# Loading the first two heads of k through SyncE, with a new order of the steps

## The chip, the core and the metric

The kernel runs on one core of one Trainium2 chip. A core has a matrix engine (TensorE, PE in the profile; its weight loads are listed apart as PEld), a vector engine (VectorE, DVE), a scalar engine (ScalarE, ACT), GpSimd (POOL) and SyncE (SP), which only issues transfers here. Each engine works through its own list of instructions in order; semaphores tie the lists together. Transfers are issued by GpSimd or by SyncE and carried by 16 DMA engines. In this kernel the transfers that GpSimd issues also change float32 into bfloat16 on the way.

The metric is the device time of one execution in microseconds (us), lower is better. Times are medians over several runs; the profile is of one execution.

## What is computed

Attention over a window and over block summaries, for 4 batches of 8 heads, 768 positions and 64 numbers a head, and behind it a feed-forward layer on the 3072 resulting rows of 512:

```python
def _attn_ref(q, k, v):
    block, window = (32, 16)
    k_sum = k.reshape(B, H, nb, block, D).max(axis=3)
    v_sum = v.reshape(B, H, nb, block, D).mean(axis=3)
    scores_l = scale * np.matmul(q, k.transpose(0, 1, 3, 2))
    mask_l = np.abs(pos[:, None] - pos[None, :]) < window
    scores_s = scale * np.einsum('bhsd,bhnd->bhsn', q, k_sum) + np.log(block)
    scores_all = np.concatenate([np.where(mask_l, scores_l, -1e9), scores_s], axis=-1)
    a = softmax(scores_all)
    return np.matmul(a, np.concatenate([v, v_sum], axis=2))

def _moe_ref(x, w_in, w_out):
    h = x @ w_in                                   # 512 -> 2048
    return (h * np.clip(h + 3.0, 0.0, 6.0) / 6.0) @ w_out
```

All inputs and the output are float32; the kernel computes in bfloat16 with float32 sums.

## The kernel before, in words

**Work.** The queries of a head are cut into 12 blocks of 64; a block sees a window of 96 keys and 24 block summaries, 120 keys in all. Heads are taken in pairs p = 0 to 3. The feed-forward part works on eight tiles of 384 rows (two halves of each batch): the F groups (line 666) multiply a tile by one of 16 column blocks of `w_in`, four matmuls of 384 columns each; ScalarE and VectorE make the gate from the result (lines 670 and 671); the G groups (line 683) multiply by `w_out`; a copy and a store by SyncE end them (lines 694 and 695).

**An order written out.** The functions only declare steps to a planner, `Plan`, with what each reads and writes. The string `ORDER` then lists every step once, by its key: the tag of the group and a number within it. A suffix `:A` or `:D` puts a step on ScalarE or VectorE. Since each engine's list is in order, this string fixes what stands behind what on every engine. `Plan.issue` walks it, gives each step its buffers (the free one that was released longest ago) and emits the instructions. Tokens that begin with `_`, `-`, `~` or `=` are filler for TensorE, emitted by `keep` (line 771): matmuls on the constant tile `idle` whose result nobody reads. `_40` is 40 matmuls of 64 columns, `-15` is 15 of 128, `~12` is 12 of 512, `=3` is one of 3 x 64 columns.

**The opening of batch 0.** These are the groups that the change and the prediction speak of:

- `c.n`: constants. c.0 is `idle`, c.1 the identity and c.2 the band (both on GpSimd), c.3 the bias for masking (`negative`), c.4 the mask, c.5 the indicator for block sums, c.6 and c.7 edges of `vaug`, c.8 to c.15 zeroed parts of `vaug`, c.16 and c.17 to c.20 edges of the sums and of `kaug`. All but c.1, c.2 and those of c.8 to c.15 that carry `:A` are VectorE's.
- `K00`, `K01`, `K02`: k of head pair 0, of pair 1 and of pairs 2 and 3, loaded by GpSimd into `knat`, a view of the tile `first` (`load_k`, line 303). `Q00`, `Q01`: half of q of pairs 0 and 1, and of 2 and 3 (line 309). `V00` to `V03`: v of one pair each (line 339). `Q0w0` to `Q0w2`: the other half of q, into `qwide` (line 316). `I0`, `I2`, `I4`, `I8`, `I12`: column blocks of `w_in`. `O0` to `O3`: `w_out`.
- `kp.0`: TensorE turns k of pair p by 16 transposes (line 391); `kp.1` takes the block maxima (line 402) and `kp.4` spreads them (line 407), both on VectorE; `kp.2` and `kp.3` copy the turned keys into `kaug`. `q0` and `q1` do the same for q (line 420), `q2` and `q3` for the half in `qwide` (line 441).
- `s0p0.0`: a matmul with the bias that opens the masked scores of pair p, first half of the queries (line 481, "cover"); `s0p0.1` the scores (line 489), `s0p0.2` the exponential. `s0p1` are the scores of the other half, which need `q2` and `q3`.
- `u0`, `u1`: block sums of v for two pairs each (line 535). `h000` and so on (batch, pair, half) are copies of v between blocks. `v0p`: values of pair p (line 581), their division by the sums, transposes (line 589) and the copy into the input tile of the first F groups.

The later batches (1 to 3) are loaded by GpSimd while the feed-forward groups of earlier tiles run. The loads of batch 2 reuse the tile `first`, so `load_raw` makes them wait for the readers of `knat` and `qnat` (`free`, line 337).

`ot` is a pool of four float32 buffers of 128 x 512, from which the output is stored.

Of the kernel before, what the change touches and what calls it, by code (L numbers as in the profile page):

```python
# [15 lines left out]
D = 64  # L16
# [7 lines left out]
RUN = 8  # L24
RP = 96
# [4 lines left out]
c.0 K00.0 c.7 c.17 c.6 c.8:A K01.0 c.10:D c.5 c.1 _40 -15 k0.0 k0.2:A c.18 ~1 =2 k1.0 K02.0 ~12 =3 k2.0 k3.0 c.15:D c.2 c.3  # L30
s000.0 k0.3:A c.13:D c.4 c.11:A k1.1 Q00.0 q0.0 k1.4 k0.1 c.20 k1.2:A Q01.0 ~2 =5 q1.0 k0.4 k1.3:D c.9:A c.14:A c.19 k2.3:A
q0.1:A s000.1 q0.2:A =1 s010.0 s010.1 k2.2:A k3.2:D k3.3:D k3.1 V00.0 h000.0:D h001.0:D k2.1 k2.4 s000.2 ~2 =5 v00.0 V01.0 u0.0
h010.0:D s020.0 c.16 s010.2 q1.2:A u0.3:D u0.1:D u0.4:D v01.0 v01.1 v01.2 v00.1 q1.1:A V02.0 h020.0:A h021.0:A h011.0:A v00.2
s020.1 v01.3 v00.3 V03.0 u1.0 u1.3:A h030.0:D s030.0 k3.4 ~2 s030.1 u1.4:D v01.4 h031.0:D Q0w0.0 Q0w1.0 v01.5:D Q0w2.0 =1 q3.0
q3.1:D q2.0 u1.1:A u1.2:D s020.2 v02.0 v02.1 v02.2 s021.0 v02.3 s030.2 v03.0 v03.1 q2.1:A v03.2 s011.0 v03.3 v00.4 v00.5:D v02.4
s021.1 s011.1 s021.2 v03.4 v03.5:D s011.2 v02.5:A s031.0 s031.1 s001.0 s031.2 I2.0 F0x3.0 F0x3.1 F0x3.2 F0x3.3 F0x3.4 F0x3.5
I4.0 F0x6.0 F0x6.1 F0x6.2 F0x4.0 F0x4.1 F0x4.2 F0x4.3 v411.0 v411.1 F0x5.0 F0x4.4 F0x4.5 v411.2 s001.1 I8.0 u0.2:A s001.2 F0x8.0
F0x8.1 F0x8.2 F0x5.1 I0.0 F0x5.2 F0x11.0 F0x1.0 F0x11.1 F0x11.2 F0x1.1 F0x1.2 F0x1.3 F0x1.4 F0x1.5 v410.0 v410.1 F0x7.0 F0x7.1
F0x7.2 v410.2 F0x10.0 F0x10.1 I12.0 F0x13.0 F0x13.1 F0x15.0 F0x15.1 F0x13.2 F0x10.2 v411.3 v411.4:D v410.3 v410.4:A F0x15.2
F0x14.0 F0x14.1 F0x14.2 F0x9.0 F0x9.1 F0x9.2 F0x0.0 F0x0.1 F0x2.0 F0x2.1 K13.0 K10.0 c.12:A F0x0.2 K12.0 K11.0 w10.0 Q1w1.0  # L40
F1x14.0 F1x14.1 F1x14.2 F1x4.0 F1x4.1 F1x4.2 F1x2.0 F1x2.1 F1x2.2 w10.1:D F0x2.2 F0x2.3 F0x2.4 F0x12.0 F0x12.1 F0x12.2 F1x8.0
F1x8.1 F1x8.2 F1x1.0 F1x1.1 F1x1.2 F0x0.3 F0x0.4 F0x0.5 F0x2.5 F1x9.0 F1x9.1 F1x9.2 F1x5.0 F1x5.1 F1x5.2 F1x15.0 F1x15.1 w11.0
w11.2 F1x15.2 w11.3:D Q1w4.0 Q1w2.0 Q1w0.0 w10.2 w10.3:D q6.0 q6.1:A q7.0 q7.1:A F1x7.0 F1x7.1 w11.1:A F1x7.2 F1x12.0 F1x12.1
F1x12.2 O0.0 G02x0.0 Q1w5.0 Q1w3.0 q4.0 q4.1:A q5.0 q5.1:A F1x6.0 F1x6.1 F1x6.2 O1.0 G02x0.1 s100.0 s100.1 s100.3 F1x3.0 w12.0
F1x11.0 F1x11.1 w13.0 w13.2 F1x3.1 F1x11.2 w12.2 w12.1:D O2.0 G02x0.2 s101.0 s101.1 O3.0 F1x10.0 G02x0.3 G02x0.4:A w13.3:D
w13.1:A s101.3 F1x0.0 G00x0.0 G00x0.1 w12.3:D s100.2 s101.2 s100.4 V10.0 h100.0:D F1x10.1 h110.0:A F1x10.2 F1x3.2 s110.0 s110.1
s110.2 s101.4 s110.3 G00x0.2 G00x0.3 G00x0.4:A V12.0 u4.0 h130.0:D h120.0:A F1x0.1 u4.1:D u4.2:A u4.4:D u4.3:D u4.5:D G02x0.5
G01x0.0 G01x0.1 G01x0.2 s110.4 F1x0.2 h111.0:A v100.0 v100.1 v100.2 h121.0:A v101.0 v101.1 v101.2 G01x0.3 G01x0.4:A K20.0 K21.0
K22.0 K30.0 K23.0 w21.0 F1x13.0 F1x13.1 F1x13.2 v100.3 v100.4:A w20.0 w21.3 G12x0.0 w21.2:A v101.3 v101.4:A V22.0 H2.0 h101.0:A
w20.3 G12x0.1 G12x0.2 F2x2.0 F2x2.1 F2x11.0 F2x2.2 F2x11.1 F2x11.2 s111.0 w23.0 s111.3 F2x1.0 F2x1.1 F2x1.2 F2x3.0 F2x3.1 F2x3.2  # L50
F2x15.0 F2x15.1 F2x15.2 Q22.0 w23.3 G12x0.3 s111.1 G12x0.4:A F2x5.0 F2x5.1 h131.0:A F2x5.2 F2x6.0 G10x0.0 s111.2 w22.0 w22.3
s111.4 w23.4:A V20.0 H2.1:A K33.0 F2x13.0 F2x13.1 F2x13.2 G10x0.1 F2x6.1 F2x0.0 F2x0.1 F2x0.2 u5.0 u5.1:A u5.5:A F2x6.2 v110.0
v111.0 v111.1 v111.2 Q30.0 F2x4.0 F2x4.1 F2x4.2 Q21.0 Q23.0 Q20.0 w22.4:A F2x10.0 F2x10.1 F2x10.2 F2x12.0 F2x12.1 w20.1 F2x12.2
w22.2:A v110.1 w21.4:A Q33.0 Q32.0 G10x0.2 G01x0.5 G10x0.3 G10x0.4:A v110.2 F2x8.0 F2x8.1 w21.1 w20.2:A F2x9.0 w20.4:A F2x9.1
F2x9.2 u5.2:D F2x14.0 u5.4:D w23.2:A F2x8.2 v111.3 F2x14.1 v111.4:A G11x0.0 G11x0.1 u5.3:D w22.1 v110.3 v110.4:A F2x7.0 F2x7.1
G11x0.2 F3x14.0 F3x14.1 F2x14.2 F2x7.2 F3x14.2 s200.0 s200.1 w23.1 w21.5:A s200.3 G11x0.3 F3x9.0 F3x9.1 F3x9.2 F3x8.0 F3x8.1
F3x8.2 F3x13.0 Q31.0 K31.0 s200.4 s200.2 G11x0.4:A G11x0.5 G12x0.5 s210.0 s210.3 s210.4 s210.1 s210.2 F3x4.0 F3x12.0 G22x0.0
F3x13.1 F3x13.2 H3.0 v201.0 K32.0 V32.0 w20.5:D F3x4.1 F3x4.2 V30.0 G00x0.5 F3x12.1 v200.0 v200.1 F3x2.0 v201.1 v201.2 v201.3
G22x0.1 F3x0.0 F3x0.1 G22x0.2 G22x0.3 w23.5:A G22x0.4:A F3x12.2 v200.2 v200.3 v201.5 F3x1.0 F3x1.1 F3x1.2 s201.0 w31.0 G20x0.0
v201.4 F3x0.2 F3x2.1 s201.3 F3x2.2 F3x11.0 s201.1 G20x0.1 F3x5.0 F3x11.1 F3x3.0 F3x5.1 F3x11.2 w30.0 F3x5.2 v201.7 F3x15.0  # L60
G20x0.2 F3x15.1 F3x15.2 w30.3 F3x3.1 F3x3.2 w22.5:A w30.4:D s201.4 F3x6.0 F3x6.1 H3.1:A G20x0.3 G20x0.4:A F3x7.0 F3x10.0 G21x0.0
s211.0 F3x7.1 F3x10.1 s201.2 F3x7.2 s211.3 s211.1 F3x10.2 w32.0 F3x6.2 w32.3 s211.4 s211.2 w30.2:A G21x0.1 G21x0.2 G21x0.3
G21x0.4:A u6.0 u6.1:D u6.5:A u6.4:A u6.2:A w31.3 v211.0 v201.6 v210.0 v210.1 v210.2 w31.2:D v211.1 v210.3 v211.2 v211.3 G10x0.5
w31.4:D w33.0 G32x0.0 G32x0.1 G32x0.2 G32x0.3 G32x0.4:A F4x14.0 F4x14.1 F4x14.2 F4x4.0 F4x4.1 w32.2:A F4x4.2 F4x15.0 F4x15.1
F4x15.2 w31.1 G30x0.0 G30x0.1 F4x8.0 F4x8.1 F4x8.2 F4x2.0 F4x2.1 F4x2.2 F4x13.0 G30x0.2 F4x13.1 u6.3:A F4x13.2 w33.3 F4x7.0
# [96 lines left out]
def kernel(  # L162
# [9 lines left out]
    nc = tc.nc  # L172
# [501 lines left out]
    def f2(s, ts, part, cols=(0, d_model)):  # L674
# [11 lines left out]
        if last:  # L686
# [116 lines left out]
```

## Time and profile before

| | us |
|---|---|
| median of 3 runs | 216.81 |
| lowest and highest run | 216.51, 218.5 |
| the profiled execution, in all | 217.01 |
| its span, first to last instruction | 215.3 |

| Engine | busy, us | share of the span |
|---|---|---|
| TensorE matmuls | 209.4 | 97% |
| TensorE weight loads | 119.6 | 56% |
| VectorE | 162.5 | 75% |
| ScalarE | 136.2 | 63% |
| GpSimd | 49.5 | 23% |

The page of a profile lists busy times by engine, the same in 40 equal slices of the span, the DMA queues, the chain of work that ended last, the costliest groups of instructions and the DMA issues. A group's row reads: line, engine, operation, what it writes <- what it reads, shapes, count, then busy time and mean duration, then the idle time before it and what ended that. In a timeline a row has start and length in us, and in brackets the idle time before it. Queue q0 carries GpSimd's transfers, q1 SyncE's:

```profile
q0 software_dynamic: 62288, 14.41, 72.2%
q1 hardware_dynamic: 29264, 7.87, 15.4%
```

The columns are packets, megabytes and the share of 16 engines' span that the packets took. Before the change the first transfer that SyncE issues is a store at 53 us.

### The profile page before, as it was taken

To read this page: it belongs to the slowest core of one execution; us is meant where nothing else is said; L and a number is where in the kernel's file an instruction comes from. 1 tells how busy PE (TensorE), PEld (TensorE's weight loads), DVE (VectorE), ACT (ScalarE), POOL (GpSimd) and SP (SyncE) were. 2 spreads that over 40 slices of the span, in tenths; PEclk is the share of its full clock that TensorE was granted. 3 is DMA by queue.
4 is the path that set the end of the run, shared out by engine and by line. 5 is a ranking of instruction groups with operands and counts; after the bars stand their busy time and mean duration, and the time that the engine had idled before them with its cause. 6 is when DMAs were issued, how large, how long until landed. Compare 5 with 4: busy or idle time off the path is not lost.

```text
span 215.3 us, 6088 instructions
## 1 busy us (share of the span) xinstructions
PE 209.4 (97%) x2548; PEld 119.6 (56%) x2548; DVE 162.5 (75%) x317; ACT 136.2 (63%) x264; POOL 49.5 (23%) x66
## 2 busy tenths in 40 slices
PE   7998999999999999999999999999999999999993
PEld 7556656555555565555555555555555555565442
DVE  6888999999899999898889888987865554640021
ACT  3887878887898988757569696466345355520110
POOL 7977358906652244000000000000000000000000
PEclk9999999999999999999999999999999999999999
DMA  5999999999999999930333233122323300013124
GB/s 74 157 152 188 203 188 170 191 204 161 205 160 192 181 134 150 104 146 12 37 43 137 28 38 107 49 24 32 73 56 48 73 0 29 23 49 122 52 70 150
DMA packets 91580, 22.68 MB, mean 105 GB/s; under 512 B 82208, under 2 KB 88608, under 8 KB 91552
## 3 DMA queue, kind: packets, MB, share of 16 engines
q0 software_dynamic: 62288, 14.41, 72.2%
q1 hardware_dynamic: 29264, 7.87, 15.4%
q8 instruction: 20, 0.33, 0.6%
q14 instruction: 8, 0.07, 0.1%
HBM read 28.82 MB, written 6.29 MB: 163 GB/s over the span
## 4 chain that ended last, share of the span: by engine, by line
PE 86%; DMA 7%; POOL 2%; ACT 2%; DVE 1%; issue 1%; ACTq 0%; POOLq 0%
PE h L666 38%; PE o L683 33%; PE h L683 5%; DMA qwide<-in_q_dram 4%; DMA first<-in_q_dram 3%; PE S L623 3%; PE S L512 3%; PE S L553 1%; ACT vaug L241 1%; POOL first L305 1%; PE S L636 1%; PE S L439 1%; PE S L666 1%; PE h L581 1%; DVE g L671 0%
## 5 line engine op out<-in xcount | busy, mean ns | idle before, releaser
L666 PE MATMUL h<-x,win 128*128 128x384 bf16 x500 | 91.1, 326 | 0.2 <-DVE g L671 0.2
L670 ACT ACTIVATE r<-h 128x384 f32<-128x384 f32 x125 | 58.8, 492 | 38.7 <-PE h L666 36.7
L671 DVE SCALAR_TENSOR_TENSOR g<-r,h 128x384 bf16<-128x384 f32 x125 | 65.7, 546 | 22.7 <-ACT r L670 20.1
L683 PE MATMUL o<-wout,g 128*128 128x512 bf16 x336 | 81.7, 379 | 0.0
L666 PEld LDWEIGHTS <-win 128*128 128x128 bf16 x512 | 48.7, 98 | 35.8 <-issue 0.4
L683 PEld LDWEIGHTS <-g 128*128 128x128 bf16 x400 | 38.4, 98 | 37.6 <-issue 0.3
L520 ACT ACTIVATE at<-S 120x768 bf16<-120x768 f32 x24 | 18.6, 811 | 5.5 <-PE S L512 5.4
L241 ACT COPY ot<-o 128x512 f32<-128x512 f32 x17 | 10.0, 586 | 16.3 <-PE o L683 15.1
L521 DVE TENSOR_TENSOR at<-at,mask 96x768 bf16<-96x768 bf16 x24 | 12.6, 549 | 2.0 <-ACT at L520 1.6
L605 DVE TENSOR_TENSOR xn<-S,rc 128x768 bf16<-128x768 f32 x14 | 13.3, 949 | 0.3
L241 DVE COPY ot<-h 128x512 f32<-128x512 f32 x2 | 1.3, 686 | 14.1 <-PE h L683 14.1
L343 POOL DMA_DIRECT2D vaug<-in_v_dram x10 | 11.8, 1187 | 0.3 <-issue 0.2
L683 PE MATMUL h<-wout,g 128*128 128x256 bf16 (+1 forms) x64 | 11.4, 326 | 0.0
L467 DVE TENSOR_REDUCE red<-kaug 128x24 bf16<-128x768 bf16 x12 | 11.2, 941 | 0.1
L241 ACT COPY vaug<-vs 24x1536 bf16<-24x1536 bf16 x6 | 8.8, 1468 | 0.6 <-DVE vs L241 0.5
L241 ACT COPY vaug<-vaug 32x640 bf16<-32x640 bf16 (+3 forms) x17 | 8.9, 574 | 0.3 <-PE S L553 0.2
L771 PE MATMUL o<-idle 128*128 128x64 bf16 (+2 forms) x70 | 7.4, 286 | 1.1 <-DVE idle L287 1.1
L455 DVE STREAM_TRANSPOSE kaug<-kraw 128x768 bf16<-128x768 bf16 x8 | 8.1, 1020 | 0.3 <-PE S L512 0.3
L333 POOL DMA_DIRECT2D kraw<-in_k_dram x8 | 5.9, 741 | 9.1 <-DVE kaug L455 7.3
L642 DVE STREAM_TRANSPOSE y<-xn 128x768 bf16<-128x768 bf16 x8 | 7.6, 965 | 0.2
L512 PEld LDWEIGHTS <-kaug 32*128 32x128 bf16 x576 | 5.3, 92 | 4.4 <-issue 3.6
L623 PEld LDWEIGHTS <-at 120*64 120x64 bf16 x336 | 6.2, 111 | 2.6 <-issue 1.5
(106 smaller groups left out, 184.2 us busy)
## 6 DMA issues: line engine op xcount, KB each, us to landing
out_dram<-ot SPq DMA_DIRECT2D x19, 256.0 KB, 2.3
vaug<-in_v_dram POOLq DMA_DIRECT2D x6, 384.0 KB, 12.9
wout<-in_moe_w_out_dram POOLq DMA_DIRECT2D x4, 512.0 KB, 9.9
win<-in_moe_w_in_dram POOLq DMA_DIRECT2D x3, 512.0 KB, 10.7
kraw<-in_k_dram POOLq DMA_DIRECT2D x8, 192.0 KB, 12.7
x<-y SPq DMA_DIRECT2D x64, 24.0 KB, 2.0
first<-in_k_dram POOLq DMA_DIRECT2D x6, 192.0 KB, 12.4
first<-in_q_dram POOLq DMA_DIRECT2D x6, 192.0 KB, 12.3
```

Source lines behind the costliest of these rows:

```text
L241: {"ACT": nc.scalar.copy, "DVE": nc.vector.tensor_copy, "POOL": nc.gpsimd.tensor_copy}[eng](o, i)
L343: op("POOL", "dma128", lambda: nc.gpsimd.dma_start(out=o[BLK:WIN, a:z, 0:D], in_=rows[:, a:z]), w=[("v", b % 2, c) for c in range(lo, hi)] ...
L467: op("DVE", "max", lambda: nc.vector.tensor_reduce(red.slot[:], w[:, :, BLK:WIN].rearrange("p t (n c) -> p t n c", n=2), axis=AX.X, op=ALU ...
L512: nc.tensor.matmul(X[g // 2].slot[:, g % 2, i * QB:(i + 1) * QB], kaug[2 * u + m][rows, t], qT[rows, 2 * u + m, t * QB:(t + 1) * QB], star ...
L520: op("ACT", "exp", lambda a=a, e=e: nc.scalar.activation(a, X[e].slot[0:KEYS, :, 0:HALF], AF.Exp, scale=scl), r=[X[e]], w=[("at", p, half)])
L521: op("DVE", "masking", lambda m=m: nc.vector.tensor_tensor(m, m, mask[:, low(half):low(half) + HQ].unsqueeze(1).to_broadcast([WIN, 2, HQ, ...
L605: nc.vector.tensor_tensor(o, src[..., 0:D], r.unsqueeze(len(r.shape)).to_broadcast(list(o.shape)), op=ALU.mult)
L623: nc.tensor.matmul(X.slot[64 * c:64 * c + 64, i, m:m + D + 1], a[:, t * QB:(t + 1) * QB], vaug[b % 2][0:KEYS, h, t, 0:D + 1], start=True, ...
L666: nc.tensor.matmul(bank(h)[:, 0:HALF], w_in_sb[:, kt, cols], xt[s].slot[:, kt], start=(kt == 0), stop=(kt == NP - 1))
L670: op("ACT", "relu", lambda: nc.scalar.activation(r.slot[:], bank(h)[:, 0:HALF], AF.Relu, bias=0.5, scale=1.0 / 6.0), r=[h], w=[r])
L671: op("DVE", "gate", lambda: nc.vector.scalar_tensor_tensor(gt[s].slot[:, ft], r.slot[:], 1.0, bank(h)[:, 0:HALF], op0=ALU.min, op1=ALU.mul ...
L683: nc.tensor.matmul(o.slot[:, a:z], gt[s].slot[:, ft, ts * 128:(ts + 1) * 128], w_out_sb[:, ft, a:z], start=(ft == 0), stop=(ft == NFT - 1))
```

## The change

k of pair 0 (the first two heads) is no longer loaded by GpSimd. SyncE loads each of the two heads in float32, unchanged, into a buffer of the pool `ot` (96 partitions of 512 numbers, 192 KB a head), and two new steps, K00.1 and K00.2, copy it into `knat` as bfloat16. Both are put on VectorE by the new order. The transposes k0.0 wait for these casts instead of the transfer, and the loads of batch 2 into the same place wait for the readers of the casts' result too.

```diff
+    def load_k_first():
+        plan.at("K00")
+        given = [Buf("ot"), Buf("ot")]
+        def go():
+            for j in range(2):
+                nc.sync.dma_start(out=given[j].slot[0:RP], in_=k[0, j].rearrange("(p s) d -> p (s d)", s=RUN))
+        op("SP", "kfirst", go, w=given, size=2)
+        for j in range(2):
+            op(EITHER, "kcast", lambda eng, j=j: copy(eng, knat[:, j].rearrange("p s d -> p (s d)"), given[j].slot[0:RP]), r=[given[j]], w=[("kc", j)])
...
-                   free=[(n, p) for p in range(NP) for n in ("kn", "qn")] if b == 2 else ...
+                   free=[("kc", 0)] + [(n, p) for p in range(NP) for n in ("kn", "qn")] if b == 2 else ...
...
-        op("PE", "ktr", tr, r=[("kn", p), "ident"], w=[T])
+        op("PE", "ktr", tr, r=[*([("kn", p)] if p else [("kc", 0), ("kc", 1)]), "ident"], w=[T])
...
     load_q(0)
-    load_k(0, 1)
+    load_k_first()
     load_k(1, 2)
```

The string `ORDER` is replaced as a whole. It lists the same steps and the two new ones. Its beginning, before:

```
c.0 K00.0 c.7 c.17 c.6 c.8:A K01.0 c.10:D c.5 c.1 _40 -15 k0.0 k0.2:A c.18 ~1 =2 k1.0 K02.0 ~12 =3 k2.0 k3.0 c.15:D c.2 c.3
s000.0 k0.3:A c.13:D c.4 c.11:A k1.1 Q00.0 q0.0 k1.4 k0.1 c.20 k1.2:A Q01.0 ~2 =5 q1.0 k0.4 k1.3:D c.9:A c.14:A c.19 k2.3:A
q0.1:A s000.1 q0.2:A =1 s010.0 s010.1 k2.2:A k3.2:D k3.3:D k3.1 V00.0 h000.0:D h001.0:D k2.1 k2.4 s000.2 ~2 =5 v00.0 V01.0 u0.0
h010.0:D s020.0 c.16 s010.2 q1.2:A u0.3:D u0.1:D u0.4:D v01.0 v01.1 v01.2 v00.1 q1.1:A V02.0 h020.0:A h021.0:A h011.0:A v00.2
s020.1 v01.3 v00.3 V03.0 u1.0 u1.3:A h030.0:D s030.0 k3.4 ~2 s030.1 u1.4:D v01.4 h031.0:D Q0w0.0 Q0w1.0 v01.5:D Q0w2.0 =1 q3.0
```

and after:

```
c.0 c.19 c.5 K01.0 c.20 c.7 c.6 c.10:D c.8:A c.14:A Q00.0 c.13:A c.15:D c.16 c.9:A c.17 K00.0 c.18 K00.1:D c.1 K02.0 K00.2:D _40
-15 k1.0 k1.2:A c.2 c.4 c.3 k0.0 q0.0 q0.1:A k0.1 k0.2:A q0.2:A k0.4 k0.3:A s010.0 k1.1 s000.0 k1.4 ~6 =3 s010.1 k1.3:D s000.1
s000.2 c.11:D k3.0 k3.3:A s010.2 k2.0 k2.1 k3.1 k2.2:A Q01.0 =5 q1.0 q1.2:A k3.2:A V00.0 h000.0:D k2.3:D k2.4 s030.0 V01.0 ~7 =1
u0.0 u0.3:A v00.0 h010.0:D =6 v01.0 v01.1 u0.1:A V02.0 h020.0:A h021.0:A q1.1:D k3.4 v01.2 u0.4:D v00.1 v00.2 v00.3 s020.0
s020.1 s020.2 v01.3 s030.1 V03.0 u1.0 v00.4 h011.0:D u1.1:A v00.5:D u1.2:D u1.3:A u1.4:D v01.4 Q0w2.0 Q0w0.0 Q0w1.0 ~3 =6 q3.0
```

So GpSimd's first loads become K01, Q00, K02, Q01, V00 in place of K00, K01, K02, Q00, Q01, V00. Behind the opening the F groups of the first tile begin with column block 4 instead of 3, the weights come as I4, I0, I2, I8, I12 instead of I2, I4, I8, I0, I12, and the rest of the string, through all eight tiles, is rearranged as well. Of the fillers, two now stand behind q3.0 (`=6` and `=4`); before, none did.

More of the change, by code (lines that the diff above doesn't have):

```diff
@@ L29 @@
 ORDER = """
[L30 to L65, printed above, removed]
@@ L86 @@
+G70x0.2 G61x0.1 G61x0.2 G61x0.3 G61x0.4:A G21x0.5 G72x0.0 G72x0.1 G72x0.2 G72x0.3 G60x0.0 G60x0.1 G70x0.3 G70x0.4:D G60x0.2
+G60x0.3 G61x0.5 G72x0.4:A G72x0.5 G70x0.5 G60x0.4:D G60x0.5 G71x0.2 G71x0.3 G71x0.4:A G71x0.5
 """
@@ L336, in load_raw @@
                    w=[(name + "r", b % 2, g)], size=768,
-                   free=[(n, p) for p in range(NP) for n in ("kn", "qn")] if b == 2 else [("qw", 1, u) for u in range(NS)] if b == 3 else ())
+                   free=[("kc", 0)] + [(n, p) for p in range(NP) for n in ("kn", "qn")] if b == 2 else [("qw", 1, u) for u in range(NS)] if b == 3 else ())
     def load_v(b, lo, hi):
```

69 lines of the change are left out of this document (49 added, 20 removed).

## The prediction

> **What bounds the kernel now.** I read the page of the profiled execution first: the engines, the slices, the chain.
>
> ```profile
> span 215.3 us, 6088 instructions
> ...
> PE 209.4 (97%) x2548; PEld 119.6 (56%) x2548; DVE 162.5 (75%) x317; ACT 136.2 (63%) x264; POOL 49.5 (23%) x66
> ...
> DMA  5999999999999999930333233122323300013124
> ...
> PE 86%; DMA 7%; POOL 2%; ACT 2%; DVE 1%; issue 1%; ACTq 0%; POOLq 0%
> ```
>
> TensorE is busy for 209.4 of 215.3 us and carries 86% of the chain, so the end moves only with what TensorE does not compute. The DMA engines are full from the second slice (5.4 us each) to about 97 us. That busy time includes matmuls on the constant `idle` tile (line 771). The windows view for that tile alone (columns: stretch, length, then PE, PEld, DVE and ACT busy, clock, DMA) and the chain in order of time say where TensorE lacks work:
>
> ```profile
> 20.00:25.00 5.00, 0.00 (x0) 0.00 (x0) 0.00 (x0) 0.00 (x0) 1.00 1.25 206
> sum 25.00, PE 9.89 PEld 5.79 DVE 0.17 ACT 3.25; mean PE 1.98 PEld 1.16 DVE 0.03 ACT 0.65
> ```
>
> ```profile
> 5.42 6.78 DMA first<-in_q_dram
> ...
> 12.48 7.88 DMA qwide<-in_q_dram
> ...
> 20.40 0.73 PE h L441 x10
> ...
> 24.33 2.06 PE h L666 x12
> ```
>
> All 9.89 us of filler lie ahead of 20 us. The chain up to there is two loads, the second landing at 12.48 + 7.88 = 20.36 us; from then on it is matmul after matmul. So I split the span at one instruction, the ten transposes of line 441 at 20.40 us (token q3.0 of the order). What follows is TensorE's own work; what precedes is an opening that waits for loads. The change acts on the opening.
>
> **The change, part by part.** These rows show the opening's marks on TensorE and the loads (timeline; then answers of the DMA view for single issues, their last number the time from issue to landing):
>
> ```profile
> 12.70 0.35 PE L489 MATMUL S<-qT,kaug 64*128 64x64 bf16 x12
> ...
> 14.71 0.85 PE L535 MATMUL o<-vaug,ind 96*32 96x128 bf16 x24
> ...
> 19.27 0.23 PEld L489 LDWEIGHTS <-kaug 64*128 64x128 bf16 x12 [0.70 <-DVE kaug L407]
> ...
> 19.76 0.28 PE L441 MATMUL h<-ident,qwide 128*128 128x128 bf16 x2
> ...
> 20.40 0.73 PE L441 MATMUL h<-ident,qwide 128*128 128x128 bf16 x10 [0.37 <-DMA qwide<-in_q_dram]
> ```
>
> ```profile
> 1.36 1.42 POOL L305 DMA_DIRECT2D first<-in_k_dram  x2 [0.84 <-POOLq L787]
> ...
> 6.08 3.76 POOL L343 DMA_DIRECT2D vaug<-in_v_dram  x4
> ...
> 9.58 0.53 PE L391 MATMUL h<-ident,first 96*64 96x96 bf16 x16
> ```
>
> ```profile
> first<-in_k_dram POOLq DMA_DIRECT2D x1, 192.0 KB, 3.3
> ...
> first<-in_k_dram POOLq DMA_DIRECT2D x1, 192.0 KB, 4.0
> ...
> vaug<-in_v_dram POOLq DMA_DIRECT2D x1, 192.0 KB, 7.0
> ...
> DMA packets 0, 0.00 MB, mean 0 GB/s; under 512 B 0, under 2 KB 0, under 8 KB 0
> ```
>
> *Removed: K00 from GpSimd's queue.* GpSimd saves one issue of 1.42 / 2 = 0.71 us. More counts that its loads come one behind another. K00 lands at 1.36 + 3.3 = 4.7, K01 at about 2.1 + 4.0 = 6.1, so K00's share of that stream is 1.4 us. The last row is the stretch from 0 to 2.8 us: no packet at all. Moving K00 to SyncE gains up to 1.4 us for every later load if its packets run in that empty stretch. Whether they can is bounded by SyncE's rows: the queue's first wait, then two stores of 256 KB, one at 212 us beside nothing, one at 64 us beside a full software queue:
>
> ```profile
> SPq L787 <- PEq L787: 0.8, 1, 0.8
> ```
>
> ```profile
> out_dram<-ot SPq DMA_DIRECT2D x1, 256.0 KB, 2.1
> ...
> out_dram<-ot SPq DMA_DIRECT2D x1, 256.0 KB, 6.0
> ```
>
> SyncE is free at 0.8 us, so K00's two halves land at about 3 to 3.5 us by the first row and at 7 by the second. Nothing else is moving before 2.8, so I take the first, and for the stream's gain 1.4 us. The last qwide load then lands at 20.36 - 1.4 = 19.0 instead of 20.36, and V01 (issue at 6.08 + 0.94, landing 14.0) at 12.6.
>
> *Added: two casts of 96x512 from float32 on VectorE, in its opening list.* No such cast is in the trace. The nearest rows are below: a copy of 512 float32 columns from PSUM at 686 ns above, 384 bf16 columns at 343 ns below. A gain is excluded, since both are new work. I take 0.55 each, nearer the float32 row.
>
> ```profile
> 3.89 0.70 DVE L282 MEMSET vaug<- 32x768 f32 x1
> ```
>
> ```profile
> L402 DVE TENSOR_REDUCE red<-h 128x24 bf16<-128x768 bf16 x3 | 2.8, 949 | 0.3 <-PE h L391 0.3
> L407 DVE COPY kaug<-red 128x288 bf16<-128x288 bf16 x4 | 1.2, 300 | 0.1
> L264 DVE COPY mask<-band 96x768 bf16<-96x768 bf16 x1 | 0.4, 442 | 0.0
> L300 DVE MEMSET kaug<- 128x48 uint32 x4 | 0.4, 98 | 0.1
> L261 DVE TENSOR_SCALAR bias<-band 96x384 bf16<-96x384 bf16 x1 | 0.3, 255 | 0.3 <-POOL band L257 0.3
> L241 DVE COPY x<-h 128x384 bf16<-128x384 bf16 x2 | 0.7, 343 | 0.0
> ```
>
> ```profile
> L241 DVE COPY ot<-h 128x512 f32<-128x512 f32 x2 | 1.3, 686 | 14.1 <-PE h L683 14.1
> ```
>
> VectorE's list up to the first cast is the constants that ended at 3.89 + 0.70 = 4.6 before, plus two of the 98 ns memsets and one smaller: 4.8 us. With landings at 3 to 3.5 the casts do not wait: they end at 4.8 + 1.1 = 5.9. Behind them in VectorE's queue stand mask and bias (0.44 + 0.26, and three small memsets, 0.9 together): 6.8. Then maximum and spread of heads 0 to 3, 2 x (0.95 + 0.3) = 2.5: 9.3 us. Only then may TensorE compute the first scores (s010.1). They were at 12.70 because Q00 and Q01 stood behind K02; Q00 now goes second, in K01's old place, with landing near 6.1, so that it no longer decides.
>
> *Moved: TensorE's own list.* From 9.3: two scores of 0.35, two transposes of k at 0.53, one keep-alive and one transpose of q together 0.7, one cover of 768 columns, then seven keep-alives of 512 columns and one of 64. A row of 1,344 filler columns prices a column:
>
> ```profile
> 13.73 0.74 PE L771 MATMUL h<-idle 128*128 128x512 bf16 x3
> ```
>
> 0.55 ns, so cover 0.4 and filler 2.0; as a row's duration includes the drain of the last matmul, I take 1.6. The sums of v (u0.0) start at 9.3 + 0.7 + 1.1 + 0.7 + 0.4 + 1.6 = 13.8, where V01 has been there since 12.6; before it was 14.71. From there to q3.0 it was 19.76 - 14.71 = 5.0 us. The new list has twelve value matmuls (0.35), three transposes (0.28) and 1,216 filler columns (0.67) more, a cover (0.42) less, and does not meet the 0.70 us wait for VectorE at 19.27, of which 0.3 was not filled: 5.6. TensorE reaches q3.0 at 13.8 + 5.6 = 19.4, a little behind the load's 19.0. It was passed at 20.40: 1.0 us gained.
>
> *After q3.0.* The new order puts two more fillers there (640 columns, 0.35) and has done three transposes earlier (0.28): 0.1 lost. The new order of the weights (I4, I0, I2 for I2, I4) asks nothing of them earlier than they come: F0x4 needs I4, whose 512 KB now go first. The rest of the reordering I cost at nothing: the cover is that loads run ahead of use there, and the price without it is one for one, since TensorE has no slack. The tail keeps its shape, a half-width copy and store last.
>
> **Sum.** -1.0 + 0.1 = -0.9 us. The profiled execution took 217.0 us (span 215.3 and 1.7 around it), so it becomes 216.1; it lies 0.2 above the median of 216.8, so I forecast **215.9 us**. By the bounds of the cast (0.34 to 0.69, two of them) and of the stream (gain 1.4, or 0.7 if K00's packets half overlap it), this case runs from 215.1 to 216.5.
>
> **Rivals.**
>
> *No gain in the stream.* K00's packets take the same engines as GpSimd's loads, so that what leaves one queue only comes back through the other: qwide lands at 20.4 as before, q3.0 stays, and the time is 216.8. For it: the DMA slices are full from the second on. Against it: the empty 2.8 us at the start. The Trainium skill says just this ("DMA: Bandwidth & Descriptors", section "Issuing engines are not separate DMA queues"): all queues run on the same 16 engines, and issuing from several saves only issue time. By that rule alone the change would be worth at most the 0.71 us of issue, and the trace agrees that the engines are shared, in that a store beside a full queue took 6.0 us against 2.1.
>
> *K00 late, slower.* SyncE's packets wait behind the software queue's as the store at 64 us did: the second half, issued at 1.2, lands at 7.2. The first cast stands at the head of VectorE's in-order list, and mask, bias and maxima queue behind it; q3.0 moves by 7.2 - 4.8 = 2.4 to 21.8, which is 1.4 later than before: 218.3. It decides from a landing of 4.8 us on. Against it: at 0.8 us that queue is empty.
>
> *TensorE's slow start lasts longer, slower.* The first fillers show that it starts at half pace though the granted clock reads 1.00:
>
> ```profile
> L771 PE MATMUL o<-idle 128*128 128x64 bf16 x40 | 2.3, 242 | 1.1 <-DVE idle L287 1.1
> ```
>
> 2,560 columns in 2.3 us are 0.9 ns each against 0.55 later. If standing still between k1.0 and the covers (some 1 us in two pieces) keeps it slow for another 4 us, about 2 us are lost ahead of u0.0 and q3.0 falls at 21.4: 218.0. The Trainium skill ("TensorE: Matmul & The Clock Gate", "Part 1: The HAM clock gate") has the array start at half rate until a window of some 3.4 us was busy; the trace agrees with the start, and no run here shows a fall back.
>
> *A larger gain.* The last qwide load took 7.88 us against 7.0 of V01; without that lag it lands 0.8 earlier, at 18.2. With casts at 0.34 and fillers that cost nothing, q3.0 follows: 2.2 gained, 214.6.
>
> *A wait of the new order in the long part.* One for one; 1 to 3 us give 217 to 219. Nothing in the trace of before names its place.
>
> **Numbers.** Chances: forecast 0.52, no gain 0.16, K00 late 0.10, slow start 0.07, larger gain 0.09, later wait 0.06. One per cent is 2.2 us, about what a measurement of this kernel can tell from no change: under 214.6 or over 219.0. Faster: the larger gain and a tail of the forecast, 0.15. Slower: the worse parts of the three slower cases, 0.11. Within: 0.74. For 8 in 10 I reach from 214.6 to 218.2.
>
> **What would show it.** K00 landing before 4.8 us, first packets before 2.8, the casts at 0.34 to 0.69 us starting near 4.8; the first scores near 9.3; u0.0 near 13.8; q3.0 near 19.4 with no long wait on qwide; TensorE without gaps after that. Wrong: casts that wait for SyncE, qwide again at 20.4, fillers at half pace beyond 6 us, or idle time of TensorE after 25 us.

## The result, and the profile after

The changed kernel takes 218.61 us (median of 20 runs, 217.63 to 220.28), the kernel before 217.32 beside it (20 runs, 216.51 to 218.96): a ratio of 1.0059, interval 1.0042 to 1.0076. It is slower by 1.3 us. The profiled execution took 219.66 us (before: 217.01), so it shows a case 1 us above the changed kernel's median.

The page of the kernel after, its span, engines and chain:

```profile
span 217.9 us, 6061 instructions
...
PE 208.7 (96%) x2520; PEld 120.8 (55%) x2546; DVE 159.4 (73%) x311; ACT 137.2 (63%) x272; POOL 48.9 (22%) x65
...
PE 93%; DMA 2%; ACT 2%; issue 2%; ACTq 0%; POOLq 0%
```

The span is 2.6 us more, while TensorE's busy time is 0.7 less: TensorE stands still longer. (The 0.7 itself says little, since 26 matmuls of this execution have no record: 2520 are listed beside 2546 weight loads.) Its share of the chain rose from 86% to 93% and that of transfers fell from 7% to 2%. The opening is no longer bound by the load of qwide but by TensorE's own list. The chain in order of time (start, length, what) begins so:

```profile
1.38 4.65 DMA first<-in_k_dram
6.07 1.49 PE h L403 x32
9.59 2.72 PE h L783 x7
```

One wait for K01, then only TensorE. Its rows in the timeline (the lines behind the new function lie 12 further down than before, so L783 is the filler line):

```profile
6.07 1.49 PE L403 MATMUL h<-ident,first 96*64 96x96 bf16 x32 [1.02 <-DMA first<-in_k_dram]
...
9.38 2.93 PE L783 MATMUL h<-idle 128*128 128x512 bf16 x7
12.24 0.80 PE L501 MATMUL S<-qT,kaug 64*128 64x64 bf16 x24
...
16.45 0.85 PE L547 MATMUL h<-vaug,ind 96*32 96x128 bf16 x24
...
20.75 0.97 PE L783 MATMUL S<-idle 128*128 128x512 bf16 x4
21.56 0.50 PE L453 MATMUL S<-ident,qwide 128*128 128x128 bf16 x6
```

TensorE stood 1.02 us for K01. The filler row at 9.38 has six matmuls of 512 columns and one of 192, 3,264 columns in 2.93 us: 0.90 ns a column, half the later pace of 0.47 (e3 below). The views print a granted clock of 1.00 there, but that is no measurement: the trace's clock records begin with the step to the full clock, at 12.88 us in this execution and at 6.21 in the kernel before, and a view counts time without a record as 1.00. First scores 12.24, sums of v 16.45, q3.0 at 21.56 with no wait for qwide, which had landed at 19.78 (12.41 + 7.4 in the row below). In this execution the opening is 1.16 us longer than before (21.56 against 20.40).

What the transfers did. The rows are single issues (the last number is the time to landing): a half of K00, K01, V01, V03 and the last of qwide, issued at 1.27, 1.38, 6.53, 8.39 and 12.41:

```profile
ot<-in_k_dram SPq DMA_DIRECT2D x1, 192.0 KB, 2.7
...
first<-in_k_dram POOLq DMA_DIRECT2D x1, 192.0 KB, 4.6
...
vaug<-in_v_dram POOLq DMA_DIRECT2D x1, 192.0 KB, 8.1
...
vaug<-in_v_dram POOLq DMA_DIRECT2D x1, 192.0 KB, 8.8
...
qwide<-in_q_dram POOLq DMA_DIRECT2D x1, 128.0 KB, 7.4
```

K00 is there at 4.0, near the forecast. But K01, which took K00's place at the head of GpSimd's queue, lands at 6.0 and not at 4.7; V01 at 14.7 (before 14.0), V03 at 17.2 (before 16.6). GpSimd's stream has one load less, and these loads are not earlier. The last qwide is, at 19.78 in place of 20.36, but by no more than the same load differs between executions with the same route (table under e9). The queues (packets, MB, share of 16 engines) show where it loses: first the kernel after from 1.8 to 3.1 us and from 3.1 to 4.1, then the kernel before from 3.1 to 4.1:

```profile
q1 hardware_dynamic: 193, 0.36, 91.1%
...
q0 software_dynamic: 54, 0.06, 90.6%
q1 hardware_dynamic: 31, 0.03, 13.6%
```

```profile
q0 software_dynamic: 158, 0.16, 105.9%
```

SyncE's packets do run in the empty stretch, as forecast: 0.36 MB of the 0.39 that the two float32 halves make. But the next microsecond is lost to GpSimd. Its packets fill the engines, 90.6% of 16, and carry 0.06 MB where they carried 0.16. One takes 16 x 0.906 / 54 = 0.27 us in place of 16 x 1.059 / 158 = 0.11. So the stream's first microsecond behind K00 yields 0.10 MB less, some 0.6 us of its pace, and it begins about 0.3 later (its first packet at 3.1, before at 2.8). Without K00 the same microsecond holds 134 packets of 0.115 us (e4 below).

The second loss lies far behind the opening. TensorE and ScalarE of the kernel after near 60 us (timeline), then the same place before:

```profile
59.69 0.57 PE L565 MATMUL S<-vaug,ind 96*32 96x128 bf16 x27
61.28 0.49 PE L565 MATMUL S<-vaug,ind 96*32 96x128 bf16 x21 [1.03 <-ACT vaug L241]
...
59.79 0.59 ACT L241 COPY ot<-o 128x512 f32<-128x512 f32 x1 [0.30 <-PE o L695]
60.41 0.83 ACT L241 COPY vaug<-vaug 32x768 bf16<-32x768 bf16 x1
```

```profile
57.41 0.85 PE L553 MATMUL S<-vaug,ind 96*32 96x128 bf16 x48
...
58.30 0.83 ACT L241 COPY vaug<-vaug 32x768 bf16<-32x768 bf16 x1 [0.20 <-PE S L553]
```

These are the block sums of batch 1 (u4.0, the same tile `vaug` whose edges the copy h130 fills). Before, the sums ran in one piece and the copies followed: the tokens are `u4.0 h130.0:D h120.0:A`, so the row of ScalarE is h120, and h130 ran on VectorE (0.35 us, from 58.34). The new order lists h130.0 ahead of u4.0, so that the rest of the sums waits for the copy, and it puts the copy on ScalarE, where it takes 0.83 and stands behind an output copy of 0.59: TensorE idles for 1.03 us.

The account of the two profiled executions: q3.0 is 1.16 later, and from there to TensorE's end it takes 193.09 us against 191.45 (21.56 to 214.65, and 20.40 to 211.85), 1.64 more. Of that 1.03 is the wait at 60 us; two waits of 0.36 and 0.34 us at 22.8 and 28.8 against two of 0.17 and 0.18 before, and the two fillers behind q3.0, make up the rest roughly.

### The profile page after: what moved, and what is told of

It reads as the page before. It is cut to its first block, busy times and chain, and to the rows that moved or that the text cites. A ratio compares the mean times of both kernels' runs of the same rounds, so it can differ in the third digit from the quotient of the medians.

```text
span 217.9 us, 6061 instructions
## 1 busy us (share of the span) xinstructions
PE 208.7 (96%) x2520; PEld 120.8 (55%) x2546; DVE 159.4 (73%) x311; ACT 137.2 (63%) x272; POOL 48.9 (22%) x65
## 4 chain that ended last, share of the span: by engine, by line
PE 93%; DMA 2%; ACT 2%; issue 2%; ACTq 0%; POOLq 0%
PE h L678 38%; PE o L695 33%; PE h L695 5%; PE S L635 3%; PE S L524 3%; PE h L783 2%; DMA first<-in_k_dram 2%; PE S L501 1%; PE S L493 1%; PE S L648 1%; PE S L565 1%; PE h L403 1%; PE h L593 1%; ACT vaug L241 1%; PE h L547 1%
## 5 line engine op out<-in xcount | busy, mean ns | idle before, releaser
L682 ACT ACTIVATE r<-h 128x384 f32<-128x384 f32 x126 | 59.5, 492 | 35.7 <-PE h L678 34.4
L695 PE MATMUL o<-wout,g 128*128 128x512 bf16 x312 | 77.5, 379 | 1.9 <-issue 0.8
L532 ACT ACTIVATE at<-S 120x768 bf16<-120x768 f32 x24 | 18.3, 808 | 5.7 <-PE S L524 5.5
L241 ACT COPY ot<-o 128x512 f32<-128x512 f32 x18 | 10.6, 588 | 15.6 <-PE o L695 15.6
L533 DVE TENSOR_TENSOR at<-at,mask 96x768 bf16<-96x768 bf16 x24 | 12.6, 547 | 1.9 <-ACT at L532 1.6
L241 DVE COPY ot<-h 128x512 f32<-128x512 f32 x1 | 0.7, 692 | 16.2 <-PE h L695 16.2
L241 ACT COPY vaug<-vaug 32x768 bf16<-32x768 bf16 (+3 forms) x17 | 9.7, 612 | 0.2
L507 ACT ACTIVATE at<-S 120x768 bf16<-120x768 f32 x8 | 6.4, 814 | 3.4 <-PE S L501 3.3
L783 PEld LDWEIGHTS <-idle 128*128 128x128 bf16 x78 | 6.2, 129 | 4.1 <-issue 1.7
```

The source lines that it names most:

```text
L241: {"ACT": nc.scalar.copy, "DVE": nc.vector.tensor_copy, "POOL": nc.gpsimd.tensor_copy}[eng](o, i)
L532: op("ACT", "exp", lambda a=a, e=e: nc.scalar.activation(a, X[e].slot[0:KEYS, :, 0:HALF], AF.Exp, scale=scl), r=[X[e]], w=[("at", p, half)])
L533: op("DVE", "masking", lambda m=m: nc.vector.tensor_tensor(m, m, mask[:, low(half):low(half) + HQ].unsqueeze(1).to_broadcast([WIN, 2, HQ, ...
L682: op("ACT", "relu", lambda: nc.scalar.activation(r.slot[:], bank(h)[:, 0:HALF], AF.Relu, bias=0.5, scale=1.0 / 6.0), r=[h], w=[r])
L695: nc.tensor.matmul(o.slot[:, a:z], gt[s].slot[:, ft, ts * 128:(ts + 1) * 128], w_out_sb[:, ft, a:z], start=(ft == 0), stop=(ft == NFT - 1))
```

## The experiments

Every one was run beside the kernel before on the same chip. Orders are shown as the tokens that differ.

**e1, the load alone.** The order of the kernel before, K00 by SyncE and the two casts.

```diff
-c.10:D c.5 c.1 _40
+c.10:D c.5 K00.1:D K00.2:D c.1 _40
```

> The load of k's first two heads through SyncE and its two casts, in the order of before (casts on VectorE ahead of k0.0). Pace theory (TensorE stood still 1.0 us for K01 and so ran at half pace until 12 us): here k0.0 comes first and its k lands at 4.0, so there is no long stand; full pace by about 6.5 us, sums of v (u0.0) at 14.7 or earlier, time within 0.5 us of before. Stream theory (SyncE's packets take the engines from GpSimd's loads): K01 still lands at 6.0 and V01 at 14.7 instead of 14.0, 0.3 to 0.7 us slower than before. Later-order theory (the waits at 28 and 60 us): they are gone, within 0.5 us of before whatever the opening does.

Measured 217.13 us, ratio 1.0012 (0.9985 to 1.0039). V01 landed at 14.57, V03 at 17.08 and the last qwide at 19.64, none clearly earlier than before. The load by SyncE with its casts neither wins nor loses anything that these runs can tell.

**e2, the order alone.** K00 by GpSimd in bfloat16 at the head of its queue, no casts, and otherwise the new order.

```diff
-c.0 c.19 c.5 K01.0 ... K00.0 c.18 K00.1:D c.1 K02.0 K00.2:D _40
+c.0 K00.0 c.19 c.5 K01.0 ... c.18 c.1 K02.0 _40
```

> The order of after, with K00 loaded by GpSimd as before, ahead of K01, and no casts. Pace theory: k1.0 is still TensorE's first step and K01 lands at 6.1, so TensorE stands still as long and stays at half pace to about 12 us: as slow as after, 1.0 to 1.6 us over before. Stream theory: V01 lands at 14.0 as before and the opening is 0.6 us faster than after's. Later-order theory: the wait at 60 us (1.0 us) is there, so at least 1 us over before.

Measured 220.0 us, ratio 1.0117 (1.0080 to 1.0154): the new order alone is worse than the whole change. V01 landed at 14.71, no earlier than after, where 14.0 was expected. The half pace until 12 us did not come either: TensorE stood for K01 even longer than in the kernel after, and the transposes behind the stand ran at full pace (0.87 us in place of 1.49), since the full clock came at 5.69 us, during the stand:

```profile
6.55 0.87 PE L391 MATMUL h<-ident,first 96*64 96x96 bf16 x32 [1.50 <-DMA first<-in_k_dram]
```

What this profiled execution (221.21 us) lost, it lost later, by an accident that no other trace shows in this size. TensorE in the timeline, then the windows (stretch, length, PE, PEld, DVE, ACT, POOL busy, granted clock, DMA):

```profile
15.51 0.22 PE L581 MATMUL h<-vaug,at 96*64 96x65 bf16 x2
17.90 0.35 PE L581 MATMUL h<-vaug,at 96*64 96x65 bf16 x10 [2.17 <-issue]
```

```profile
16.00:18.00 2.00, 0.10 (x6) 0.10 (x8) 1.14 (x3) 1.81 (x4) 0.74 (x1) 1.00 2.43 151
18.00:20.00 2.00, 2.00 (x51) 1.11 (x53) 0.76 (x3) 0.00 (x0) 1.90 (x3) 0.84 1.79 184
20.00:22.00 2.00, 2.00 (x49) 1.81 (x48) 1.53 (x4) 0.81 (x1) 2.00 (x3) 0.50 1.30 207
22.00:24.00 2.00, 2.00 (x22) 1.48 (x19) 1.32 (x3) 1.73 (x4) 0.95 (x2) 0.81 1.43 197
```

TensorE stood for 2.17 us with no wait that the profile shows, and the granted clock then fell to half: by the clock records for 3.41 us, from 19.34. One such stretch makes a mean granted clock of 0.992 over a run (1 - 0.5 x 3.41 / 216). Five of its six runs have 0.992 or less, where the kernel after has 6 of 20.

**e3, more filler ahead of k1.0** in the kernel after, so that TensorE does not stand while K01 comes.

```diff
-_40 -15 k1.0
+_40 -27 k1.0
```

> After, with 27 instead of 15 fillers of 128 columns ahead of k1.0, so that TensorE does not stand still between 5.0 and 6.1 us. Pace theory: full pace by 6.5 to 9 us, first scores near 10.4 instead of 12.24, u0.0 near 14.8 instead of 16.45, q3.0 near 19.9 instead of 21.56, 1.3 to 1.7 us faster than after. Stream theory and later-order theory: u0.0 and q3.0 within 0.3 us of after's, no change of the time.

Measured 217.92 us, ratio 1.0032 (1.0004 to 1.0061). TensorE in the timeline:

```profile
8.48 1.54 PE L783 MATMUL h<-idle 128*128 128x512 bf16 x7
...
14.99 0.83 PE L547 MATMUL h<-vaug,ind 96*32 96x128 bf16 x23 [0.71 <-DMA vaug<-in_v_dram]
...
20.06 0.50 PE L453 MATMUL S<-ident,qwide 128*128 128x128 bf16 x6
```

The same filler row takes 1.54 us in place of 2.93, the scores come at 9.96, and TensorE now waits for V01, as it was meant to. q3.0 falls at 20.06, when the last qwide lands (20.02): the opening is back at what the loads allow. The 1.50 us that q3.0 gains are what was expected (1.3 to 1.7); of the time only some 0.6 us came, by the ratios. This trace does not show that the fillers did it: its full clock came at 4.80 us, when TensorE was still at the fillers that the kernel after has too (they end there at 5.04).

**e4, K00 not loaded.** ScalarE fills the two buffers with zeros instead, so the output is not attention over the given k. It shows what the stream would be if K00 cost it nothing. (K00.0, now a step of ScalarE, also moves to behind c.0 in the order.)

```diff
-                nc.sync.dma_start(out=given[j].slot[0:RP], in_=k[0, j]...)
+                nc.scalar.activation(given[j].slot[0:RP], idle[0:RP, 0:1].to_broadcast([RP, 512]), AF.Copy, scale=0.0)
```

> After, with k of the first two heads not loaded at all: ScalarE fills the two buffers with zeros in its opening, and the casts read those. Stream theory: K01 lands at 4.7 instead of 6.0, K02 at 9 to 9.5 instead of 11.2, V01 at 12.6 to 13 instead of 14.7, and q3.0 falls near 19.4; 2 us faster than after. If SyncE's packets do not disturb the stream: K01 lands at 6.0 and V01 at 14.7 again, and TensorE stands still as long as in after. Pace theory adds only that full pace comes by 6.5 us wherever K01 lands before 5.2.

Measured 216.97 us, ratio 0.9978 (0.9958 to 0.9999). K01 and the last qwide, issued at 1.38 and 11.66:

```profile
first<-in_k_dram POOLq DMA_DIRECT2D x1, 192.0 KB, 3.5
...
qwide<-in_q_dram POOLq DMA_DIRECT2D x1, 128.0 KB, 6.6
```

K01 lands at 4.9 and the last qwide at 18.3. These are about the times that the prediction had given to the stream with K00 in SyncE's queue (K01's 6.1 less 1.4, so 4.7, and 19.0 for the last qwide). So the forecast gain belongs to a load that does not happen. GpSimd's packets from 3.1 to 4.1 us are short again, 16 x 0.963 / 134 = 0.115 us each:

```profile
q0 software_dynamic: 134, 0.14, 96.3%
```

TensorE also does not stand for K01, and q3.0 falls at 18.30, 2.10 earlier than before. By the ratios this version is 1.8 us under the kernel after, near the expected 2. Even so the time is only 0.2% under the kernel before: from q3.0 to its end TensorE takes 193.44 us in place of 191.45. The wait of 1.03 us (at 58.37) is half of these 1.99; waits of 0.39 and 0.35 at 19.5 and 25.9 are part of the rest, which was not traced further.

**e5, the sums first**: u4.0 ahead of the copy h130, otherwise the kernel after.

```diff
-V12.0 h130.0:A V10.0 u4.0 u4.1:A
+V12.0 V10.0 u4.0 h130.0:A u4.1:A
```

> After, with the sums of batch 1 (u4.0) moved ahead of the halo copy h130 in the order, so that TensorE does not wait there for ScalarE. Later-order theory: the 1.03 us wait at 60 us goes, nothing else takes its place, 0.8 to 1.1 us faster than after. Opening theories (pace, stream): the time lost lies ahead of q3.0, and this changes nothing or is taken back by the next wait: within 0.3 us of after.

Measured 218.3 us, ratio 1.0030 (0.9993 to 1.0066).

```profile
59.03 0.85 PE L565 MATMUL S<-vaug,ind 96*32 96x128 bf16 x48
```

The sums run in one piece again, with no wait. The gain is 0.3%, some 0.6 us by the ratios, less than the expected 0.8 to 1.1. In this execution the full clock came at 5.77 us with an unchanged opening, where it came at 12.88 in the kernel after, and the same transposes ran at full pace behind a stand of nearly the same length:

```profile
5.96 0.87 PE L403 MATMUL h<-ident,first 96*64 96x96 bf16 x32 [0.91 <-DMA first<-in_k_dram]
```

The pace differs from execution to execution.

**e6, both**: the 27 fillers and the sums first.

> Both edits: 27 fillers ahead of k1.0 and u4.0 ahead of h130. If the two losses are separate they add: 0.7 + 1.0 us faster than after, 0.2 to 0.5 us faster than before. If one hides the other: no better than the better of the two alone.

Measured 217.3 us, ratio 0.9997 (0.9970 to 1.0024). The whole loss is gone, and nothing is gained, where 0.2 to 0.5 us under before had been expected if the two add. In ratios to the kernel before, the filler takes 0.27% off 0.59%, the sums 0.29%, both 0.62%: about 0.6 us each. The intervals of e3 and e5 overlap that of the kernel after; that of e6 does not. The other versions say the same of the sums: with the fillers and the wait the ratios are 1.0032 and 1.0031 (e3, e8), with the fillers and the sums first 0.9997, 0.9997 and 1.0002 (e6, e10, e11).

**e7, less filler in the kernel before**, to see what the slow pace costs there.

```diff
-_40 -15 k0.0
+_40 -5 k0.0
```

> Before, with 5 instead of 15 fillers of 128 columns ahead of k0.0, so that TensorE stands still for about 1 us until K00 lands at 4.7. Pace theory: full pace comes some 3 us later than 6.8 us, at 9 to 10.5 (the 512-column fillers then take 0.43 us each). The first scores wait for q at 12.2 anyway, so the time stays within 0.5 us of before. If the pace has nothing to do with standing still: full pace by 6.8 us as before.

Measured 217.4 us, ratio 1.0000 (0.9970 to 1.0029). Its fillers while K02 comes, and below the same thirteen in the kernel before:

```profile
7.04 4.15 PE L771 MATMUL o<-idle 128*128 128x512 bf16 x13
```

```profile
6.80 2.85 PE L771 MATMUL o<-idle 128*128 128x512 bf16 x13
```

TensorE stood 0.85 us, the full clock came at 9.71 us, and the median is the same (its interval leaves some 0.6 us either way). In the old order the loads decide, and most of the 1.3 us of slower TensorE disappears in the waits for them: in this execution 0.6 of it is left at q3.0, which falls at 20.99 and no longer waits for qwide (landed at 19.60), in place of 20.40.

**e8, the order alone with 27 fillers** (e2 with `-27`).

> The order of after with K00 loaded by GpSimd, as in the order-alone run, and 27 fillers ahead of k1.0. There TensorE stood 2.2 us at v00.0 with no wait in the profile, while its instruction packet came at 15.5 us instead of about 10, and lost its pace behind it. If that stand belongs to when instructions are fetched: with 24 more instructions ahead the packet comes near 10 again, no stand, q3.0 at 20.2 to 20.6, and the time is before's plus the later wait, 0.9 to 1.3 us over before. If it belongs to the order's own dependencies: the stand stays, and the time is within 0.5 us of the order-alone run's.

Measured 218.16 us, ratio 1.0031 (1.0006 to 1.0057).

```profile
15.72 0.83 PE L535 MATMUL h<-vaug,ind 96*32 96x128 bf16 x23 [0.65 <-DMA vaug<-in_v_dram]
...
60.01 0.49 PE L553 MATMUL S<-vaug,ind 96*32 96x128 bf16 x21 [1.02 <-ACT vaug L241]
```

The accident of e2 is gone, twelve of twelve runs have a full clock, and the wait at 60 us remains. The first packet of the instruction queue came at 11.9 us and q3.0 fell at 20.79; the time is 0.7 us over before by the ratio, a little less than the expected 0.9. This is e3's ratio, with K00 in the other queue: again the route of the load makes no difference.

**e9, K00 in float32 through GpSimd**, at the head of its queue, casts kept.

```diff
-                nc.sync.dma_start(out=given[j].slot[0:RP], ...)
+                nc.gpsimd.dma_start(out=given[j].slot[0:RP], ...)
```

> The kernel after, but the two float32 loads of K00 are issued by GpSimd at the head of its own queue; the casts stay. It separates two causes for the stream not being relieved: V03 landed at 16.57 us in the kernel before (K00 as bfloat16 at the head of GpSimd's queue), at 17.21 in the kernel after (float32 through SyncE), at 15.74 with K00 not loaded. If the float32 bytes written are the cause, V03 lands at 17.0 to 17.4 again. If the sharing of the engines by two queues is the cause, V03 lands near 16.6, as before, or a second issue of 0.7 us later. Time: K00's second half lands at 5 to 6 us, K01 at 6.5 to 7.5, later than in the kernel after, so TensorE's stand for K01 grows by 0.5 to 1.5 us; ratio to before 1.004 to 1.011.

Measured 220.23 us (4 runs), ratio 1.0149 (1.0105 to 1.0193), above the expected 1.011; why it exceeds that is not settled, its profiled execution took 219.55. V03 landed at 17.06 (issued at 9.59, 7.5 later), in the expected band for the bytes. The landings of all profiled executions, however, spread too widely to part bytes from queues:

| K00 | V03 landed, us | last qwide landed, us |
|---|---|---|
| SyncE, float32 (after, e1, e3, e5, e6, e10, e11) | 17.21, 17.08, 17.49, 16.70, 17.24, 17.34, 16.75 | 19.78, 19.64, 20.02, 19.25, 19.81, 19.92, 20.44 |
| GpSimd, bfloat16 (before, e7, e2, e8) | 16.57, 17.03, 17.82, 18.23 | 20.36, 19.60, 20.20, 20.81 |
| GpSimd, float32 (e9) | 17.06 | 19.62 |
| not loaded (e4) | 15.74 | 18.30 |

What stands out is only the last row, a single execution: whoever carries K00, the stream pays for it.

**e10 and e11, fewer fillers.** e10 is e6 without the fillers ahead of q3.0 and without the two behind it; e11 leaves out only the two behind.

```diff
-Q0w1.0 ~3 =6 q3.0
+Q0w1.0 q3.0
...
-h001.0:D =6 v03.4
+h001.0:D v03.4
...
-s011.0 =4 s031.0
+s011.0 s031.0
```

> As e6_filler_and_sums, without the fillers ahead of q3.0 (~3 =6) and the two behind it (=6, =4): 1,536 + 384 columns ahead, 640 behind. If those behind only keep TensorE busy in time that it would otherwise have used for values, scores and F groups, they cost 0.55 ns a column: 0.35 us less than e6, ratio 0.997 to 0.9985. If TensorE waits there for ScalarE or for a load anyway, the time stays at e6's 217.3 and the ratio at 0.999 to 1.001, with the idle time shown in place of the fillers. If TensorE falls to a lower clock or pace without them, the opening lengthens by 0.5 us or more and the ratio is above 1.001.

> As e6_filler_and_sums, without the two fillers behind q3.0 (=6 and =4, 640 columns) but with those ahead of it (~3 =6) kept. In e10, without both, six of twelve runs had a mean granted clock of 0.992 and a median of 217.82 us, the six others 216.97; in e6 one run of twelve. If the fillers ahead of q3.0 are what keeps the clock, at most two of twelve runs here show a mean clock under 0.994, and the time is e6's less up to 0.35 us (640 columns at 0.55 ns): ratio to before 0.997 to 0.9995. If those behind q3.0 keep it, five or more runs show the lower clock and the ratio is 0.9995 to 1.002. If the fillers behind q3.0 only stand in time in which TensorE would wait for ScalarE, the clock stays and so does e6's time of 217.3.

Measured: e10 217.3 us, ratio 0.9997 (0.9976 to 1.0019); e11 217.27, ratio 1.0002 (0.9983 to 1.0022). Neither is faster than e6. e10's timeline and windows:

```profile
19.96 0.45 PE L453 MATMUL S<-ident,qwide 128*128 128x128 bf16 x5 [0.54 <-DMA qwide<-in_q_dram]
...
21.44 0.38 PE L593 MATMUL h<-vaug,at 96*64 96x65 bf16 x12 [0.69 <-DVE qT L241]
```

```profile
20.00:22.00 2.00, 1.30 (x35) 1.19 (x35) 1.56 (x4) 1.99 (x4) 1.74 (x3) 1.00 1.36 200
22.00:24.00 2.00, 2.00 (x62) 1.56 (x56) 1.73 (x5) 1.23 (x4) 0.78 (x1) 0.76 1.41 199
24.00:26.00 2.00, 2.00 (x31) 1.27 (x30) 1.61 (x5) 1.62 (x3) 1.25 (x3) 0.50 1.25 208
26.00:28.00 2.00, 2.00 (x33) 1.15 (x31) 1.32 (x3) 1.43 (x4) 0.29 (x2) 0.89 1.25 204
```

Without the fillers TensorE waits for qwide and for the copy of q in pieces of 0.54 and 0.69 us, and the clock falls to half behind them. Six of e10's twelve runs have a mean clock of 0.992 (their median 217.82), six of 0.998 or more (216.97). In e11 two of twelve have the lower one, in e6 one. These counts, six of twelve against three of 24, point to the fillers ahead of q3.0 as what keeps the clock; what is saved without them where it holds is lost again where it does not. That e11 gains nothing for its 640 columns fits the load: in its profile TensorE waits at q3.0 for qwide:

```profile
20.48 0.45 PE L453 MATMUL S<-ident,qwide 128*128 128x128 bf16 x5 [0.91 <-DMA qwide<-in_q_dram]
```

No version tried that loads k beats the kernel before.

## Why the prediction was wrong

**The step that failed first: "for the stream's gain 1.4 us".** K00's landing (3 to 3.5 us forecast; 3.5 and 4.0 measured for the halves, ahead of the casts) was near enough and the empty stretch was right: nearly all its packets ran ahead of 3.1 us. The inference from there, that what runs in an empty stretch costs the other queue nothing, was wrong: GpSimd's packets began later and took 0.27 us each for the next microsecond in place of 0.11 (0.115 with K00 left out). K01 landed at 6.0, 1.1 us later than with K00 left out, V01 at 14.7 in place of the forecast 12.6, the last qwide at 19.8 in place of 19.0. The lower bound that the prediction set, half the gain, was still too good for V01 and V03, which came 0.6 later than before. Why the packets are slower there is not settled: in e9 too, where GpSimd alone carries the same float32 load, the loads behind it are no earlier. (The DMA row that the prediction read is full to about 91 us, not 97; nothing rests on it.) The rival "no gain in the stream" held, and with it the Trainium skill's rule that it quoted ("DMA: Bandwidth & Descriptors", section "Issuing engines are not separate DMA queues"): the four profiled executions with K00 as bfloat16 in GpSimd's queue and the seven with SyncE agree with it, in that their loads land in the same band.

**The casts: right.** VectorE's row in the kernel after:

```profile
4.84 0.86 DVE L241 CAST first<-ot 96x512 bf16<-96x512 f32 x2
```

They start at 4.84 (forecast 4.8) and take 0.43 each (forecast 0.55, bounds 0.34 and 0.69). They wait for nothing; "K00 late" did not happen.

**"From 9.3: two scores", and 0.55 ns a column: wrong.** The step counted VectorE's queue as what ends last and took the full pace for granted. K01, now the first thing that TensorE needs, landed so late that TensorE waited 1.02 us for it, which follows from the first step (in e4 it landed at 4.91 and there was no wait), and the half pace lasted to 12.88, so that a column of the fillers ahead of the first scores cost 0.90 instead of 0.55. First scores 12.24 in place of 9.3, u0.0 16.45 in place of 13.8. In e5, with the same opening and the full clock at 5.77, they came at 9.67 and 14.17, near the forecast: what the step lacked is the pace. The rival "slow start" named the effect and the size (q3.0 at 21.4; measured 21.56) with a chance of 7 in 100; that the two figures meet so closely is in part luck, since the same opening gave 20.23 in e5. From u0.0 on the list cost 5.1 us, near the 5.6 of the working.

Whether the stand is what lengthens the slow pace stays open. The full clock came late in three of the thirteen profiled executions (after 12.88, e9 10.37, e7 9.71), and all three had stood for 0.85 to 1.08 us between 3.9 and 6.2 us. Eight executions had stood for no more than 0.24 us by then and had the full clock between 4.35 and 6.64. But e2 and e5 had stood too and had it at 5.69 and 5.77. So a stand goes with a late full clock in some executions and not in others. For the 12 more fillers speak only the times: 0.27% from after to e3 and 0.33% from e5 to e6, in the same direction, each within the noise. The medians pay less for the pace (0.6 us) than the profiled execution (1.16).

**"The rest of the reordering I cost at nothing: the cover is that loads run ahead of use there": wrong.** The cover looked at loads only. The wait at 60 us is for a copy on ScalarE, which the new order put ahead of the sums that need it. The rival "a wait of the new order in the long part" came true, at 1.03 us of its 1 to 3 and with a chance of 6 in 100. "One for one" fits in size but is not shown: e5 removes 1.03 us of idle time in the profile and 0.6 in the ratio, and from q3.0 to TensorE's end its execution took 192.99 us against 193.09, as other waits stood in the place of this one. The diff shows the tokens `h130.0:A V10.0 u4.0`; they would have had to be compared with the old `u4.0 h130.0:D`.

**The sum.** Forecast for the profiled execution: -1.0 + 0.1. Measured: +1.16 + 1.64 at TensorE's end. The two profiled executions lie 1.05 us above and 0.31 under their medians; by the medians it is +1.3, in halves of about 0.6 from the opening and from the wait, neither of which a single comparison shows clear of the noise. Without both (e6) the answer is the rival "no gain": 217.3, the time before. So of the 2.2 us between the forecast -0.9 and the measured +1.3, 0.9 is the gain that did not come and 1.3 the two losses.

## What to carry to other kernels

When a load is moved to another queue, an empty stretch is no proof of a gain: here 0.36 of 0.39 MB ran in one, and the loads behind it landed no earlier. Leave the load out once (e4) to see what it can be worth at most, and read the landings of the loads behind it. When an order is rewritten, look at each step that copies into a tile ahead of a matmul on it, and at what stands ahead of that copy on its engine. Where TensorE waits in several pieces close together, filling them can be worth more than the waits, because the clock fell to half behind such pieces in e10. An opening bound by loads can hide most of a slower TensorE (0.7 of 1.3 us in e7's trace).

## What was unexpected of the hardware

- The granted clock of the views says nothing about the start: the clock records of a trace begin with the step to the full clock, and ahead of it 1.00 is printed while the pace is half (0.90 ns a column in the kernel after, 0.47 in e3 for the same 3,264 columns, which took 1.54 us). The step stood at 4.35 us in e1 and at 12.88 in the kernel after. The Trainium skill ("TensorE: Matmul & The Clock Gate", "Part 1: The HAM clock gate") has the moment differ between runs, which the executions here agree with (5.77 us in e5, 12.88 in the kernel after, by the same opening).
- Short stands were followed by a clock of one half, for 3.41 us each time: 2.17 us in e2, and two pieces of 0.54 and 0.69 us in e10. Single stands of 0.9 us (e6, e11) and of 1.03 us at 60 us (the kernel after) were not. The same page, section "Why this matters for your kernels", puts the limit at idle gaps of about 3 us; these runs differ from it.
- TensorE stood with no wait in the profile for 2.17 us in e2, 0.84 in e5 and 0.90 in e6. In e2 the first packet of the instruction queue came at 15.5 us, where the other executions have it between 9.4 and 14.2 (e5 at 13.6, e6 at 12.1). That TensorE waited there for instructions behind the full queue of transfers is argued only; no run isolates it.
